# Column sums of a LayerNorm backward: from TensorE products per tile to running sums on GpSimd

## The chip, the cores and the metric

The kernel runs on one core of a Trainium2 chip. The metric is the device time of one execution in microseconds (us), here as the median of several runs. The engines are named as in the profile: PE is TensorE (PEld its weight loads), DVE is VectorE, ACT is ScalarE, POOL is GpSimd, SP is SyncE, which here only issues DMAs.

## The reference

One transformer-like block and its whole backward pass: a recurrent-memory attention (64 segments of 32 rows with 8 memory rows, 32 heads of 128) and a gated feed-forward part, each behind a LayerNorm whose shift, scale and gate come from a conditioning vector `c`.

```
mod = (silu(c) @ w_mod).reshape(c.shape[0], 6, 1, -1)
sa, ca, ga, sb, cb, gb = mod[:, 0], mod[:, 1], ...
h = layernorm(x) * (1 + ca) + sa
x = x + ga * A_ref(h, A_mem0, A_Wq, A_Wk, A_Wv, A_Wo)
h = layernorm(x) * (1 + cb) + sb
x = x + gb * B_ref(h, B_w_gate, B_w_up, B_w_down)
# outputs: x, and the gradients of all differentiable inputs
```

The part that matters here is the gradient of `sa` and `ca`. With `dh` the gradient of the first `h` (2048 rows of 512), they are sums over all rows: `dsa = sum(dh)` and `dca = sum(dh * xhat)`, where `xhat` is the normalised `x`. With the other four they make the six rows of `dmod`, from which the gradients of `w_mod` (output 11) and `c` (output 10) follow.

## The kernel before, in words

The kernel has phases 0 to 5. Phases 0 to 4 do the forward pass and the backward pass through the two parts. Phase 5 is the last stage: `phase5`, from about 2425 us to the end. It does two things side by side.

The first is the weight gradients of the attention. The list `todo` holds 36 chunks: 9 each for Wo, Wq, Wk and Wv, and each chunk covers `ng` = 4, 3, 4, 4, 3, 4, 4, ... heads (per group of 11, 11 and 10 heads: 4, 4 and 3, twice, then 4, 4 and 2). For Wo a chunk has one group of 20 products (128x128 by 128x512) for each head (L2195). For the other three a chunk has four groups of 20 products with `ng` x 128 columns (L2180). A group accumulates in one PSUM buffer out of six (`psG`, tag "p"), is evacuated by DVE and ACT in turn into one of three `ot` (or `ot5o`) buffers (L63 and L61 are the lines of the helper `evac`), and is stored by a DMA issued on POOL (L2184, L2200). The row tiles of a chunk, `rows5`, have three buffers; `load_rows(i + 2)` is issued in chunk `i`, on SP and ACT (L1984). Chunk 0's products were partly done at the end of phase 4 (L2002).

The second is the backward pass of the first LayerNorm in 16 tiles of 128 rows. `ln_load` loads `x0`, `dhb` and `dx1` on SP (two buffers each). `ln_tile(j)` computes the statistics on DVE, `rstd` on POOL (L2069), `xh` on DVE (L2071), the product `pr` = `dhb` * `xh` on POOL (L2074), the row gradient on DVE and ACT in `ln_bwd_rows` (L2219 to L2235), and its cast and store on POOL (L2078, L2079). `ln_step` calls it ahead of chunks 6 to 29, about two tiles for three chunks. The two column sums are made on PE: L2072 multiplies the whole `dhb` tile by `sel[:, 0, :]`, a 128x128 matrix whose column 0 is ones and whose other columns are zero, and L2075 does the same for `pr` with column 1. All 32 products accumulate in one PSUM tile, `acc_ps`, whose rows 0 and 1 then hold the sums.

From chunk 30 on `mod_grads` finishes: step 0 copies the two rows (`accs`, L2088), writes them to the DRAM tensor `DMOD` (L2089) and loads all of `DMOD` back, broadcast to 128 partitions (`dmod_bc`, L2091); steps 1 to 4 make `w_mod`'s gradient (L2098) and a dot product (L2101); step 5, ahead of chunk 35, makes `c`'s gradient (`dcb` L2111, a transpose on PE L2113).

The order on each engine is chosen when the kernel is built: the framework's scheduler goes by the order of the program, but may let an engine do a later instruction early if that one is ready in its model. So in the trace DVE and POOL work on a tile some tens of microseconds ahead of the chunk at which it stands in the program, while PE keeps the program's order. On SP the program's order is pinned up to chunk 5. Semaphore waits between engines, and those for the reuse of a buffer, are set by the framework. An engine works through its queue strictly in order, so an instruction that waits holds all behind it.

Of the kernel before, what the change touches and what calls it, by code (L numbers as in the profile page):

```python
# [7 lines left out]
BF16 = mybir.dt.bfloat16  # L8
F32 = mybir.dt.float32
AF = mybir.ActivationFunctionType  # L10
ALU = mybir.AluOpType
# [29 lines left out]
class K:  # L41
# [1971 lines left out]
    def phase5(self):  # L2013
        nc, tc, cfg, io = self.nc, self.tc, self.cfg, self.io
        D, DC, H, E, L, M, T, NS, NT, G = cfg.D, cfg.DC, cfg.H, cfg.E, cfg.L, cfg.M, cfg.T, cfg.NS, cfg.NT, cfg.G
# [6 lines left out]
        with ExitStack() as ctx:  # L2022
# [7 lines left out]
            wp = ctx.enter_context(tc.tile_pool(name="p5a_w", bufs=1, reuse_waits="tile"))  # L2030
# [1 line left out]
            sb2 = ctx.enter_context(tc.tile_pool(name="p5a_s2", bufs=2, reuse_waits="tile"))  # L2032
            psAcc = ctx.enter_context(tc.tile_pool(name="p5a_psAcc", bufs=1, space=PSUM, reuse_waits="tile"))
            ca1_bc = wp.tile([128, D], F32, name="ca1_bc")
            sel = wp.tile([128, 2, 128], BF16, name="sel5")
            nc.vector.memset(sel[:], 0.0)
            for i in range(2):
                nc.vector.memset(sel[:, i, i:i + 1], 1.0)
            mhalf = wp.tile([128, 1], F32, name="mhalf5")
            nc.gpsimd.memset(mhalf[:], -0.5)  # L2040
            acc_ps = psAcc.tile([128, D], F32, name="acc5_ps")

            ln_in = {}

            def ln_load(j):
                if j >= NT or j in ln_in:
                    return
                r0, r1 = j * 128, (j + 1) * 128
                x0 = sb2.tile([128, D], BF16, name="x0_5")
                nc.sync.dma_start(x0[:], x_rows[r0:r1, :])  # L2050
                dhb = sb2.tile([128, D], BF16, name="dhb5")
                self.load_x_rows(dhb, j, self.DHA, self.DHB)
                dx1 = sb2.tile([128, D], F32, name="dx1_5")
                nc.sync.dma_start(dx1[:], self.DX1ROWS[r0:r1, :])
                ln_in[j] = x0, dhb, dx1

            def ln_tile(j):
                r0, r1 = j * 128, (j + 1) * 128
                ln_load(j)
                ln_load(j + 1)  # L2060
                x0, dhb, dx1 = ln_in.pop(j)
                st = sb1.tile([128, 6], F32, name="st5")
                nc.vector.bn_stats(st[:], x0[:])
                mv = sb1.tile([128, 2], F32, name="mv5")
                nc.vector.bn_aggr(mv[:], st[:])
                ve = sb1.tile([128, 1], F32, name="ve5")
                nc.vector.tensor_scalar_add(ve[:], mv[:, 1:2], EPS)
                rstd = sb1.tile([128, 1], F32, name="rstd5")
                nc.gpsimd.tensor_tensor(rstd[:], ve[:], mhalf[:], op=ALU.pow)  # L2069
                xh = sb1.tile([128, D], F32, name="xh5")  # L2070
                nc.vector.tensor_scalar(xh[:], x0[:], mv[:, 0:1], rstd[:, 0:1], op0=ALU.subtract, op1=ALU.mult)  # L2071
                nc.tensor.matmul(acc_ps[:, :], lhsT=sel[:, 0, :], rhs=dhb[:], start=(j == 0), stop=False)  # L2072
                pr = sb2.tile([128, D], BF16, name="pr5")
                nc.gpsimd.tensor_tensor(pr[:], dhb[:], xh[:], op=ALU.mult)  # L2074
                nc.tensor.matmul(acc_ps[:, :], lhsT=sel[:, 1, :], rhs=pr[:], start=False, stop=(j == NT - 1))  # L2075
                dx0 = self.ln_bwd_rows(sb1, dhb, ca1_bc, xh, rstd, dx1, name="dx0")
                dx0b = sb2.tile([128, D], BF16, name="dx0b")
                nc.gpsimd.tensor_copy(dx0b[:], dx0[:])  # L2078
                nc.gpsimd.dma_start(dx0_rows[r0:r1, :], dx0b[:])  # L2079
# [4 lines left out]

            def mod_grads(step):
                if step == 0:
                    accs = sb1.tile([2, D], F32, name="accs5")
                    nc.vector.tensor_copy(accs[:], acc_ps[0:2, :])  # L2088
                    nc.sync.dma_start(self.DMOD[0:2, :], accs[:])  # L2089
                    mg["bc"] = sbm.tile([128, 6 * D], F32, name="dmod_bc")  # L2090
                    nc.sync.dma_start(mg["bc"][:], self.DMOD[:, :].rearrange("r d -> (r d)").partition_broadcast(128))  # L2091
                    mg["dscT"] = sbm.tile([128, DC], F32, name="dscT")
                elif step <= DC:
                    cc = step - 1
                    wm = sbm.tile([128, 6 * D], BF16, name="wmod5", bufs=2)
                    nc.sync.dma_start(wm[:], io["w_mod"][cc * 128:(cc + 1) * 128, :])
                    o = sbm.tile([128, 6 * D], BF16, name="dwm")
                    nc.scalar.activation(o[:], mg["bc"][:], AF.Copy, scale=self.scT[:, cc:cc + 1])  # L2098
                    nc.sync.dma_start(io["out_11"][cc * 128:(cc + 1) * 128, :], o[:])
                    junk = sbm.tile([128, 6 * D], BF16, name="junk5")  # L2100
                    nc.vector.scalar_tensor_tensor(out=junk[:], in0=wm[:], scalar=1.0, in1=mg["bc"][:], op0=ALU.mult,  # L2101
                                                   op1=ALU.mult, accum_out=mg["dscT"][:, cc:cc + 1])
                elif step == DC + 1:
                    t1 = sbm.tile([128, DC], F32, name="dc_t1")
                    nc.vector.tensor_scalar(t1[:], self.sigc[:], -1.0, 1.0, op0=ALU.mult, op1=ALU.add)
                    nc.vector.tensor_mul(t1[:], t1[:], self.cT[:])
                    nc.vector.tensor_scalar_add(t1[:], t1[:], 1.0)
                    nc.vector.tensor_mul(t1[:], t1[:], self.sigc[:])
                    nc.vector.tensor_mul(t1[:], t1[:], mg["dscT"][:])
                    dcb = sbm.tile([128, DC], BF16, name="dcb16")  # L2110
                    nc.vector.tensor_copy(dcb[:], t1[:])  # L2111
                    dc_ps = psT.tile([DC, 128], BF16, name="dc_ps")
                    nc.tensor.transpose(dc_ps[:, :], dcb[:, :], self.ident[:, :])  # L2113
                    dc_rows = sbm.tile([DC, 128], BF16, name="dc_rows")
                    nc.vector.tensor_copy(dc_rows[:], dc_ps[:])
                    nc.sync.dma_start(io["out_10"].rearrange("o (cc p) -> (o cc) p", p=128), dc_rows[:])
# [3 lines left out]
            def ln_step():  # L2120
                if ln_done[0] < NT:
                    ln_tile(ln_done[0])
                    ln_done[0] += 1

            if not getattr(cfg, "skip_wgrad", False):
# [35 lines left out]
                for i, (_, kind, outw, (hl, g0, ng)) in enumerate(todo):  # L2161
# [6 lines left out]
                    rows = loaded.pop(i)  # L2168
# [4 lines left out]
                    if i >= n_ln:  # L2173
                        mod_grads(i - n_ln)
                    h0 = 3 * g0 + hl
                    if kind == "qkv":
                        for c in range(DC):
                            ps = psG.tile([128, 4 * E], F32, name="gps5", tag="p")
                            for tp_ in range(NTP):
                                nc.tensor.matmul(ps[:, 0:ng * E], lhsT=hrows[:, tp_, c * 128:(c + 1) * 128],  # L2180
                                                 rhs=rows[:, tp_, 0:ng * E], start=(tp_ == 0), stop=(tp_ == NTP - 1))
# [4 lines left out]
                    else:  # L2186
# [4 lines left out]
                        else:  # L2191
                            pss = [psG.tile([128, D], F32, name="gps5o", tag="p") for _ in range(ng)]
                            for gg in range(ng):
                                for n, t in enumerate(self.p5_order):
                                    nc.tensor.matmul(pss[gg][:], lhsT=rows[:, t, gg * E:(gg + 1) * E], rhs=dyrows[:, t, :],  # L2195
                                                     start=(n == 0), stop=(n == NTP - 1))
# [202 lines left out]
```

## Time and profile before

| what | value |
|---|---|
| time, median of 3 runs | 3001.38 us (2998.03, 3001.38, 3002.9) |
| span of the profiled execution, first to last instruction | 2991.0 us |
| the median above that span | 10.4 us |
| mean granted clock of PE | 0.996 |
| PE busy, whole span | 2932.8 us (98%) |
| POOL busy, whole span | 1197.2 us (40%) |
| last stage, 2425 to 2991 us: PE, DVE, ACT, POOL busy | 558.37, 143.20, 63.26, 155.72 us |

No separate device time is given for the profiled execution; its span stands in for it, and the 10.4 us lie around it or between executions. In the rows of the profile "x" is a count, "128x512 bf16<-128x512 f32" the output and the input of an instruction, and what stands behind "<-" at the end of a row is what the engine had waited for. Names lack their buffer numbers, so `dhb5` stands as `dhb`, `ot5` as `ot`.

### The profile page before, as it was taken

The numbers are of one execution on the slowest core, as the hardware profiler recorded it, in microseconds if no ns is written. First come the engines' busy times: TensorE is split into PE (matmuls) and PEld (weight loads), VectorE is DVE, ScalarE is ACT, GpSimd is POOL, SyncE is SP. The second block draws the span as 40 slices with busy tenths as digits, with TensorE's granted clock in tenths as the row PEclk, the third lists the DMA queues.
The fourth block names the chain that finished last, engine by engine and source line by source line (L and its number), as shares of the span: only waits on it lengthen the run. The fifth ranks groups of instructions, "written<-read, shape, count | busy, mean of one in ns | idle before, by whom it ended". The sixth has DMA issues, their size and how long they took to land.

```text
span 2991.0 us, 105890 instructions
## 1 busy us (share of the span) xinstructions
PE 2932.8 (98%) x43975; PEld 1839.9 (62%) x44049; DVE 1612.4 (54%) x3679; ACT 1271.8 (43%) x3057; POOL 1197.2 (40%) x2456
## 2 busy tenths in 40 slices
PE   6999999999999999999999999999999999999999
PEld 3666666666665544445677777777777754445454
DVE  5566656666655788833456665566566532222230
ACT  2555555555555533312355555555555520011111
POOL 2454555555545222221344444444444422333321
PEclk8999999999999999999999999999999999999999
DMA  9898888889889899998699999999999997766574
GB/s 310 222 223 211 214 217 217 213 214 215 217 218 277 211 230 226 229 290 278 200 251 251 251 253 243 250 250 250 255 255 250 254 281 245 242 207 214 178 245 144
DMA packets 836438, 703.05 MB, mean 235 GB/s; under 512 B 536643, under 2 KB 708851, under 8 KB 835061
## 3 DMA queue, kind: packets, MB, share of 16 engines
q1 hardware_dynamic: 710756, 486.09, 65.5%
q0 software_dynamic: 54640, 148.90, 15.7%
q10 hardware_dynamic: 70560, 61.28, 6.5%
q8 instruction: 347, 5.69, 0.8%
q14 instruction: 135, 1.10, 0.1%
HBM read 294.99 MB, written 276.35 MB: 191 GB/s over the span
## 4 chain that ended last, share of the span: by engine, by line
PE 87%; issue 5%; DMA 3%; DVE 2%; POOL 1%; ACT 1%; SPq 1%; DVEq 0%; POOLq 0%; ACTq 0%
PE pass_ps L257 14%; PE gps L2180 9%; PE dh_ps L215 8%; PE pass_ps L659 5%; PE g_ps L1810 5%; PE gps5o L2195 4%; PE dhq_ps L223 4%; PE at_ps L223 4%; PE mm L1291 3%; PE dh_tps L215 3%; PE gps L1470 3%; PE turn_ps L829 2%; PE mm L1266 2%; PE mm L1251 1%; PE tps L1727 1%
## 5 line engine op out<-in xcount | busy, mean ns | idle before, releaser
L2180 PE MATMUL gps<-rows,hrows 128*128 128x512 bf16 (+2 forms) x2125 | 415.6, 355 | 1.8
L2180 PEld LDWEIGHTS <-hrows 128*128 128x128 bf16 x2160 | 211.3, 98 | 204.5
L61 ACT ACTIVATE ot<-gps 128x512 bf16<-128x512 f32 (+3 forms) x75 | 41.3, 550 | 362.2 <-PE gps L2180 229.1
L1855 POOL COPY dOst<-RAd 96x512 bf16<-96x512 bf16 x128 | 75.3, 613 | 297.8 <-DVE RAd L63 297.8
L1038 POOL TENSOR_TENSOR Pst<-Pst,rden 120x1408 bf16<-120x1408 bf16 x63 | 159.9, 2538 | 77.8 <-issue 49.6
L659 PE MATMUL pass_ps<-Wv,hT 128*32 128x512 bf16 (+2 forms) x2304 | 187.2, 358 | 0.0
L63 DVE CAST ot<-gps 128x512 bf16<-128x512 f32 (+3 forms) x76 | 48.1, 633 | 247.0 <-PE gps L2180 169.9
L2184 POOL DMA_DIRECT2D out_dram<-ot x108 | 81.5, 755 | 249.1 <-DVE ot L63 141.9
L257 PEld LDWEIGHTS <-hT 128*32 128x32 bf16 x4096 | 114.8, 97 | 103.9 <-issue 5.7
L63 DVE CAST Vst<-pass_ps 96x512 bf16<-96x512 f32 x128 | 87.3, 682 | 107.0 <-ACT RBv L61 98.5
L215 PE MATMUL dh_ps<-WvT,dVT 128*32 128x512 bf16 x2048 | 133.3, 380 | 1.7
L659 PE MATMUL pass_ps<-Wv,hb 128*32 128x512 bf16 (+2 forms) x636 | 128.7, 353 | 0.0
L257 PE MATMUL pass_ps<-Wq,hT 128*32 128x512 bf16 x2048 | 123.9, 383 | 4.8 <-DMA Wq<-in_A_Wq_dram 4.8
L257 PE MATMUL pass_ps<-Wk,hT 128*32 128x512 bf16 x2048 | 123.2, 382 | 2.5 <-POOL hT L549 1.1
L223 PE MATMUL at_ps<-Wo,OT 128*32 128x256 bf16 x4096 | 123.9, 273 | 0.7 <-DMA Wo<-in_A_Wo_dram 0.6
L257 PE MATMUL pass_ps<-WoT,dyT 128*32 128x256 bf16 (+1 forms) x3072 | 122.5, 308 | 0.9 <-ACT dyT L1936 0.9
L223 PE MATMUL dhq_ps<-WqT,dQT 128*32 128x256 bf16 x4096 | 122.9, 273 | 0.0
L215 PE MATMUL dh_ps<-WkT,dKT 128*32 128x512 bf16 x2048 | 122.3, 380 | 0.0
L794 POOL DMA_DIRECT2D Vst<-RBv x192 | 99.9, 526 | 55.6 <-ACT ET L841 34.4
L2195 PE MATMUL gps5o<-WoT,rows 128*128 128x512 bf16 x548 | 120.6, 379 | 1.0 <-DMA rows<-OSR 0.4
L223 PEld LDWEIGHTS <-dQT 128*32 128x32 bf16 x4096 | 109.7, 97 | 15.8
L315 DVE TENSOR_TENSOR dST<-dh_ps,dST 128x512 bf16<-128x512 f32 x64 | 44.3, 692 | 129.9 <-ACT dST L314 129.9
(471 smaller groups left out, 6991.2 us busy)
## 6 DMA issues: line engine op xcount, KB each, us to landing
OSR<-Ost SPq DMA_DIRECT2D x64, 352.0 KB
OT<-OT SPq DMA_DIRECT2D x64, 352.0 KB
PS<-Pst SPq DMA_DIRECT2D x64, 352.0 KB
Pst_l<-PS SPq DMA_DIRECT2D x64, 352.0 KB
OT_l<-OT SPq DMA_DIRECT2D x64, 352.0 KB
DVR<-rows_x POOLq DMA_DIRECT2D x64, 352.0 KB, 6.3
DKR<-rows_x POOLq DMA_DIRECT2D x64, 352.0 KB, 5.7
DQR<-rows_x POOLq DMA_DIRECT2D x64, 352.0 KB, 3.4
```

Of the source, the lines that this page charges most:

```text
L63: return nc.vector.tensor_copy(out, in_)
L215: self.nc.tensor.matmul(ps[32 * j:32 * j + 32, :], lhsT=lhsT, rhs=w, start=(n < 4), stop=(n >= total - 4), tile_position=(0, 32 * j))
L223: nc.tensor.matmul(ps[32 * j:32 * j + 32, :], lhsT=x[k], rhs=w[k][:, 256 * d:256 * d + 256], start=(n == 0), stop=(n == total - 1), tile_p ...
L257: self.nc.tensor.matmul(ps[32 * j:32 * j + 32, :], lhsT=lhs(c), rhs=rhs, start=(c == 0), stop=(c == DC - 1), tile_position=(0, 32 * j))
L659: nc.tensor.matmul(ps[32 * j:32 * j + 32, o * E:(o + n) * E], lhsT=lhsT, rhs=wc[:, 3 * a + hl:3 * (a + n - 1) + hl + 1:3, :], start=(c == ...
L794: nc.gpsimd.dma_start(Vst[96 + 8 * j:104 + 8 * j, :], rb[32 * j + o:32 * j + o + 8, :])
L1038: nc.gpsimd.tensor_tensor(Pst[0:120, :, :], Pst[0:120, :, :], rden[:, :].unsqueeze(2).to_broadcast([120, G, 128]), op=ALU.mult)
L1291: nc.tensor.matmul(hp[:], lhsT=xT[:, fc, :], rhs=wT[:, fc, :], start=(n == 0), stop=(n == 2 * FC - 1))
L1470: nc.tensor.matmul(ps[:], lhsT=h2r[:, j, c * 128:(c + 1) * 128], rhs=xr[:, j, :], start=(j == 0), stop=(j == NT - 1))
L1810: nc.tensor.matmul(ps[:, j, 0:w], lhsT=lh[:, g * GW:(g + 1) * GW], rhs=rh[:, g * GW:g * GW + w], start=True, stop=True)
L2180: nc.tensor.matmul(ps[:, 0:ng * E], lhsT=hrows[:, tp_, c * 128:(c + 1) * 128], rhs=rows[:, tp_, 0:ng * E], start=(tp_ == 0), stop=(tp_ == ...
L2195: nc.tensor.matmul(pss[gg][:], lhsT=rows[:, t, gg * E:(gg + 1) * E], rhs=dyrows[:, t, :], start=(n == 0), stop=(n == NTP - 1))
```

## The change

The sums are kept by POOL in one fp32 tile, `sums5` (128 partitions x 2 x 512), which is cleared at the start of the stage. In each of the 16 LayerNorm tiles POOL adds `dhb` to the first half and `pr` to the second, elementwise, and the two products on PE are left out. When all tiles are done, step 0 of `mod_grads` makes two fp32 products, which sum the 128 partitions: `sel` is now 128x2x2 in fp32, and the output has two rows. Everything else is as before.

```diff
-            sel = wp.tile([128, 2, 128], BF16, name="sel5")
+            sel = wp.tile([128, 2, 2], F32, name="sel5")
             nc.vector.memset(sel[:], 0.0)
             for i in range(2):
                 nc.vector.memset(sel[:, i, i:i + 1], 1.0)
+            sums = wp.tile([128, 2, D], F32, name="sums5")
+            nc.gpsimd.memset(sums[:], 0.0)
...
+            def add_rows(i, rows):
+                nc.gpsimd.tensor_tensor(sums[:, i, :], sums[:, i, :], rows[:], op=ALU.add)
...
                 nc.vector.tensor_scalar(xh[:], x0[:], mv[:, 0:1], rstd[:, 0:1], op0=ALU.subtract, op1=ALU.mult)
-                nc.tensor.matmul(acc_ps[:, :], lhsT=sel[:, 0, :], rhs=dhb[:], start=(j == 0), stop=False)
+                add_rows(0, dhb)
                 pr = sb2.tile([128, D], BF16, name="pr5")
                 nc.gpsimd.tensor_tensor(pr[:], dhb[:], xh[:], op=ALU.mult)
-                nc.tensor.matmul(acc_ps[:, :], lhsT=sel[:, 1, :], rhs=pr[:], start=False, stop=(j == NT - 1))
+                add_rows(1, pr)
                 dx0 = self.ln_bwd_rows(sb1, dhb, ca1_bc, xh, rstd, dx1, name="dx0")
...
                 if step == 0:
+                    for i in range(2):
+                        nc.tensor.matmul(acc_ps[0:2, :], lhsT=sel[:, i, :], rhs=sums[:, i, :], start=(i == 0), stop=(i == 1))
                     accs = sb1.tile([2, D], F32, name="accs5")
                     nc.vector.tensor_copy(accs[:], acc_ps[0:2, :])
```

## The prediction

> **What bounds the kernel now.** I read the page's first lines, then the windows view over the last stage, the groups by line there, TensorE's (PE's) order of time, the waits, and last the stores and evacuations that could hold PE up.
>
> ```profile
> span 2991.0 us, 105890 instructions
> PE 2932.8 (98%) x43975; PEld 1839.9 (62%) x44049; DVE 1612.4 (54%) x3679; ACT 1271.8 (43%) x3057; POOL 1197.2 (40%) x2456
> 2443.20:2977.00 533.80, 531.33 (x2624) 261.26 (x2672) 139.19 (x270) 60.70 (x86) 149.02 (x197) 1.00 0.67 219
> PE gps5o L2195 <- DMA rows<-OSR: 0.4, 1, 0.4
> ```
>
> The third line is the windows row of the last stage from chunk 1 to chunk 34: length, then busy time of PE, PEld, DVE, ACT, POOL, the granted clock (1.00), DMA share and GB/s. PE is busy 531.33 of 533.80 us; POOL (GpSimd) 149.02, that is 28%. The last line is the only wait of PE that the waits view lists for the stage. So here a product less on PE is time less, as long as nothing else falls behind.
>
> ```profile
> 2443.20 77.86 PE L2195 MATMUL gps5o<-WoT,rows 128*128 128x512 bf16 x353 [0.43 <-DMA rows<-OSR]
> 2520.89 0.38 PE L2072 MATMUL acc_ps<-dhb,sel 128*128 128x512 bf16 x1
> 2521.11 0.38 PE L2075 MATMUL acc_ps<-pr,sel 128*128 128x512 bf16 x1
> 2521.32 17.43 PE L2195 MATMUL gps5o<-WoT,rows 128*128 128x512 bf16 x78
> 2583.05 30.43 PE L2180 MATMUL gps<-rows,hrows 128*128 128x512 bf16 x158
> 2613.75 17.43 PE L2180 MATMUL gps<-rows,hrows 128*128 128x512 bf16 x78
> 2881.73 0.38 PE L2072 MATMUL acc_ps<-dhb,sel 128*128 128x512 bf16 x1
> 2881.95 0.38 PE L2075 MATMUL acc_ps<-pr,sel 128*128 128x512 bf16 x1
> 2882.16 95.23 PE L2180 MATMUL gps<-rows,hrows 128*128 128x384 bf16 x472
> ```
>
> These are rows of PE's order of time: start, length, line, operation, how many. From 2443.20 to 2520.89 stand chunks 1 to 5, 18 heads of 20 products: 77.69 / 360 = 0.2158 us from one 512-column product to the next. The 0.38 of a single row is its passage through the pipeline; the two sums products start 0.22 apart and the next weight-gradient product 0.21 later. So each of them takes one full place, 0.2158 us, in a queue that has no holes.
>
> **What is removed.** 16 tiles of 2 products, 32 x 0.2158 = 6.91 us, all between 2520.89 and 2882.16. Their weight loads ran beside other products and bring nothing more. VectorE's fills of `sel` become smaller by tenths of a microsecond at the stage's start, off PE; I count nothing for them.
>
> **What PE gets back.** Two fp32 products of 512 columns ahead of chunk 30. No fp32 product stands in this trace. Bounds: as cheap as a bf16 product, 2 x 0.2158 = 0.43; or, since this kernel itself carries an fp32 value as a high and a low bf16 part (`sc_parts`), high and low of both operands, so four bf16 products in one: 8 x 0.2158 = 1.73, and if none of the eight hides its passage, 8 x 0.38 = 3.04. I take 1.73, by the kernel's own way of carrying fp32, and keep 0.43 to 3.04 for the range. The Trainium skill, page "FP8 and Floating Point Precision", section "TensorE Precision Notes", says that true FP32 takes four passes through the array; by it the sum would be the same 1.73, and no row here shows such a product.
>
> Net on PE: -6.91 + 1.73 = **-5.18 us** (from -6.48 to -3.87).
>
> **What GpSimd gets.** Two additions of 128x512 into an fp32 tile per tile of rows, 32 in all, and one clearing of 128x1024 fp32.
>
> ```profile
> L2074 POOL TENSOR_TENSOR pr<-dhb,xh x16: 1166/1608/1692, 2459.8 to 2857.4; 128x512 bf16<-128x512 bf16 x16
> L1038 POOL TENSOR_TENSOR Pst<-Pst,rden 120x1408 bf16<-120x1408 bf16 x63 | 159.9, 2538 | 77.8 <-issue 49.6 <-DMA Pst<-ET 20.6 <-POOL hT L549 6.2
> L1857 POOL MEMSET Kst<- 128x1408 bf16 x1 | 1.3, 1277 | 0.0
> 2441.20 0.54 POOL L2200 DMA_DIRECT2D out_dram<-ot5o  x1 [7.59 <-DVE ot5o L63]
> ```
>
> The first row gives min/median/max of the nearest operation: same engine and width, one bf16 and one fp32 input. The second, all bf16, gives 2538 / 1408 = 1.80 ns a column, 0.92 us at 512. I take the median of the first, 1.61 us (0.92 to 1.69): 32 x 1.61 = 51.5 us, so POOL goes to about 200 of 534 us (38%). The clearing costs 0.9 (by columns) to 1.9 us (by bytes), from the third row; POOL stands idle 7.59 us before its first store of the stage, which covers it. If that cover were gone, the first store would come under 2 us later.
>
> So POOL's sum is far from PE's; what counts is who waits behind the additions. POOL also issues every store of an `ot`/`ot5o` tile. There are three such buffers, so evacuation k waits until store k-3 has landed, and PE may not start group k+6 before evacuation k (six PSUM buffers). I worked out for all 140 groups how long an evacuation could still be late; the tightest is the first of chunk 11, `ng`=3, 384 columns:
>
> ```profile
> 2611.98 0.69 DVE L2063 BATCH_NORM_STATS2 st<-x 128x6 f32<-128x512 bf16 x1 [5.38 <-DMA x<-in_A_x_dram]
> 2612.59 0.54 DVE L63 CAST ot<-gps 128x384 bf16<-128x384 f32 x1
> 2617.45 0.49 ACT L61 ACTIVATE ot<-gps 128x384 bf16<-128x384 f32 x1 [9.89 <-DMA out_dram<-ot]
> out_dram<-ot POOLq DMA_DIRECT2D x72, 128.0 KB, 3.5
> ACT ot L61 <- DMA out_dram<-ot: 25.3, 4, 9.9
> DVE ot L63 <- DMA out_dram<-ot: 14.8, 5, 4.7
> ```
>
> Chunk 10 began at 2583.05 and takes 80 x 0.2158 = 17.26, so that group ended at 2600.31 + 20 x 0.1619 = 2603.5 (384 columns: 0.2158 x 0.75); it was evacuated by 2613.1. Its buffer is wanted again two 512-column groups after 2613.75, at 2622.4. So 9.2 us were to spare. Per tile the additions put 3.2 us ahead of the stores behind them, 3.4 at the longest. That fits, and from chunk 12 on the spare time I found is 11 us or more.
>
> **VectorE beside it.** Its work on the same tile can be held too:
>
> ```profile
> L2223 DVE SCALAR_TENSOR_TENSOR dx_junk<-dx_dxh,xh x16: 693/1524/1528, 2461.6 to 2858.1; 128x512 f32<-128x512 f32 x16
> 2583.14 1.60 POOL L2074 TENSOR_TENSOR pr<-dhb,xh 128x512 bf16<-128x512 bf16 x1 [2.92 <-PE acc_ps L2072]
> 2583.76 1.52 DVE L2223 SCALAR_TENSOR_TENSOR dx_junk<-dx_dxh,xh 128x512 f32<-128x512 f32 x1
> ```
>
> The same instruction takes 0.69 us at best and 1.52 beside a POOL operation, ending just after it. Two more POOL operations can hold two more VectorE instructions by some 0.83 us each: 1.7 us. With the 3.4 an evacuation comes at most 5.1 us later, against 9.2 to spare. I price this at nothing on PE. The Trainium skill speaks against the change here: "SBUF — State Buffer", "SBUF: two separate sides", says that VectorE operations with two SBUF inputs and GpSimd share a port pair as an exclusive lock, held for the whole instruction. By it every such pair excludes each other, and the trace agrees (1.52 against 0.69); the sum stays as it is while 5.1 is below 9.2.
>
> **Waits that go.** The wait in the second row above (POOL on an old PE product of two tiles before, 2.92 us, and one of 2.5) goes, as `pr` and `dhb` are now read on POOL alone. That gives POOL 5 us back, not PE. The loads of `dhb` on SP's queue may start earlier, never later than POOL's own reading.
>
> **The end of the sums.**
>
> ```profile
> 2857.41 1.63 POOL L2074 TENSOR_TENSOR pr<-dhb,xh 128x512 bf16<-128x512 bf16 x1 [3.89 <-DMA dhb<-DHB]
> 2882.37 0.68 DVE L2088 COPY accs<-acc_ps 2x512 f32<-2x512 f32 x1 [4.00 <-PE acc_ps L2075]
> 2883.26 0.46 SPq L2089 DMA_DIRECT2D DMOD<-accs  x1
> 2890.59 0.35 SPq L2091 DMA_DIRECT2D dmod_bc<-DMOD  x1
> 2915.87 0.17 DVE L2111 CAST dcb<-dc_t 128x4 bf16<-128x4 f32 x1
> 2977.32 0.22 PE L2113 MATMUL dc_ps<-ident,dcb 128*4 128x128 bf16 x1
> 2987.09 0.72 POOL L2184 DMA_DIRECT2D out_dram<-ot  x1 [1.37 <-ACT ot L61]
> ```
>
> The last `pr` ends at 2859.0; with two additions and a store the sums are complete by about 2864. PE reaches chunk 30 at 2882.16 + 80 x 0.1619 = 2895.1, less 6.9: 2888.2. So PE doesn't wait for GpSimd (24 us to spare). The copy `accs` now follows at about 2890, 8 us later than now. Behind it on VectorE stand evacuations: an idle VectorE up to 2890 may hold one or two groups of 384 columns for up to 8 us, of 16 (five groups of 3.24) that PE may lead. On SP's queue the round trip through `DMOD` (7.3 us from 2883.26 to 2890.59) also moves 8 us back; behind it stand the row loads of chunks 33 to 35, the first wanted at 2942 (chunks 30 and 31, 17.3 us each, and 32, 12.95, after 2895.1). The four `w_mod` steps follow, and `dcb` would be ready at about 2924, against PE's use at 2977.3 - 5.2 = 2972. Nothing of it reaches the end: after PE's last group come one evacuation and one store, as now.
>
> So the span goes from 2991.0 to 2985.8. The shown runs have a median 10.4 us above the span of the profiled execution, which I leave as it is: 3001.38 - 5.18 = **2996.2 us**.
>
> **Rivals.**
> *A, stores fall behind (slower).* With three `ot` buffers the loop evacuation, store issue, landing must turn in three groups, 3 x 4.316 = 12.95 us. At the longest wait of 9.9 with 0.69 + 0.54 + 3.2 it takes 14.3: 1.4 us too long each time. If landings were that slow at all 16 tiles, 22 us would gather, 9.2 are absorbed: +13, less 5.2: about 3009; with VectorE held as well (1.7 a tile) 16 x 3.1 - 9.2 - 5.2 = +35: 3036. It decides from about 0.9 us a tile without recovery. For it: nine waits on stores are there today (25.3 + 14.8 us). Against: the median landing is 3.5 us, at which the loop takes 7.9, and lateness falls back. Chance 0.13, mostly near the lower price.
> *B, the changed queues cost PE directly (slower).* The larger tile moves all later tiles of the stage, and queues are filled anew; PE could find one `rows` load or evacuation late per few chunks. Price: a miss as large as A's spare, 9.2, once or twice: +4 to +13, 3005 to 3015. Nothing shown speaks for it. Chance 0.07.
> *C, the saving isn't kept (same).* PE is ahead by 6.9 us and then waits as long for a `rows` load, as it did once for 0.43 us. 3001.4. Against: one such wait in 36 chunks. Chance 0.07.
>
> **How the numbers follow.** The forecast has 0.73. About 0.2% (6.0 us, to 2995.4) is what a measurement of this kernel tells from no change; the forecast's -5.18 lies 0.8 us short of it, the fp32 price moves it by +-1.3, and the shown runs differ by 4.9 us (2998.03 to 3002.9). So it falls on both sides almost evenly: 0.36 faster, 0.37 same. C and the mild ends of A and B add 0.07 + 0.03 to same; the rest, 0.17, is slower. The forecast's own range is 2996.2 with -1.3/+1.3 for the price and 2.4 for the runs: 2992.5 to 2999.9. To hold 8 in 10 it takes in C and A's beginning: 2992 to 3005.
>
> **What would show it.** PE without L2072 and L2075 and with a short fp32 group of about 1.7 us ahead of chunk 30; chunks 6 to 29 back to back; POOL's additions near 1.6 us; a busy POOL near 200 us in the stage; `accs` near 2890. It is wrong if PE's waits list an evacuation (DVE or ACT `ot`) or if the fp32 group is above 3 us.

## The result, and the profile after

The changed kernel took 2994.05 us (median of 22 runs, 2986.64 to 3005.37), the kernel before beside it 2998.19 us (22 runs, 2993.78 to 3009.0). The ratio is 0.9985 with a 95% interval of 0.9978 to 0.9992: 4.5 us faster (2.4 to 6.6), where 5.18 were forecast.

One profile alone would have misled. The profiled execution with the change has a span of 2993.6 us, 2.6 us *longer* than the 2991.0 of before. PE's order of time shows where. First before, its last group; then the last stage with the change (start, length, line, operation, count):

```profile
2977.47 8.91 PE L2180 MATMUL gps<-rows,hrows 128*128 128x256 bf16 x80
```

```profile
2450.66 121.03 PE L2202 MATMUL gps5o<-WoT,rows 128*128 128x512 bf16 x549 [1.09 <-DMA rows<-OSR]
2571.52 324.36 PE L2187 MATMUL gps<-rows,hrows 128*128 128x512 bf16 x1652
2895.82 1.88 PE L2093 MATMUL acc_ps<-sums,sel 128*2 128x512 f32 x4
2897.63 82.24 PE L2187 MATMUL gps<-rows,hrows 128*128 128x512 bf16 x392
2979.80 0.22 PE L2120 MATMUL dc_ps<-ident,dcb 128*4 128x128 bf16 x1
2979.95 8.91 PE L2187 MATMUL gps<-rows,hrows 128*128 128x256 bf16 x80
```

Chunk 1 started 7.46 us later in this execution (2450.66 against 2443.20). From there to PE's last product, called the *stretch* below, it is 2443.20 to 2986.38 = 543.18 us before and 2450.66 to 2988.86 = 538.20 with the change: 4.98 less. The two sums products between the chunks are gone, chunks 6 to 29 stand back to back, and the fp32 pair takes 1.81 us of PE (2895.82 to 2897.63). The only wait of PE that the waits view lists for the stage is the 1.09 just ahead of the stretch.

GpSimd's new work and the tile's other operations, minimum/median/maximum in ns:

```profile
L2046 POOL TENSOR_TENSOR sums<-sums,dhb x16: 1149/1167/1725, 2467.1 to 2672.0; 128x512 f32<-128x512 f32 x16
L2046 POOL TENSOR_TENSOR sums<-sums,pr x16: 1482/1490/1499, 2470.9 to 2674.4; 128x512 f32<-128x512 f32 x16
L2079 POOL TENSOR_TENSOR pr<-dhb,xh x16: 1160/1289/1617, 2469.6 to 2673.1; 128x512 bf16<-128x512 bf16 x16
L2040 POOL MEMSET sums<- x1: 951/951/951, 2442.6 to 2442.6; 128x1024 f32 x1
L2237 DVE SCALAR_TENSOR_TENSOR dx_ta<-dx_dxh,rstd,dx x16: 741/1387/3140, 2469.5 to 2675.0; 128x512 f32<-128x512 f32 x16
```

The additions cost about what was forecast. But the last `pr` starts at 2673.1, where before it was 2857.4: the 16 tiles now bunch up in the first half of the stage. The waits for their loads, before and after, say the same:

```profile
DVE dx_dxh L2219 <- DMA dhb<-DHB: 65.3, 13, 9.7
```

```profile
DVE dx_dxh L2226 <- DMA dhb<-DHB: 10.7, 2, 7.5
```

So one tile's work follows the other's closely. The tightest evacuation shows what this does:

```profile
2652.95 3.07 DVE L2230 SCALAR_TENSOR_TENSOR dx_junk<-dx_dxh,xh 128x512 f32<-128x512 f32 x1
2653.19 1.16 POOL L2046 TENSOR_TENSOR sums<-sums,dhb 128x512 f32<-128x512 f32 x1
2654.30 1.16 POOL L2079 TENSOR_TENSOR pr<-dhb,xh 128x512 bf16<-128x512 bf16 x1
2655.54 1.50 POOL L2046 TENSOR_TENSOR sums<-sums,pr 128x512 f32<-128x512 f32 x1
2656.20 0.68 DVE L63 CAST ot<-gps 128x512 bf16<-128x512 f32 x1
```

This evacuation is that of the first group of chunk 13. That group ended at 2450.66 + 880 x 0.2158 = 2640.6 (860 places of chunks 1 to 12, then 20; from chunk 0 on, `ng` is 4, 4, 3, 4, 4, 3, 4, 4, 2). It was evacuated by 2656.9, and PE wanted the buffer at 2660.0, after three groups of 512 and two of 384 columns. Spare time: 3.1 us, against 9.2 for the tightest before. VectorE's `dx_junk`, 0.69 us when alone, was held for 3.07 us: it let two GpSimd operations pass and ended 0.48 us into the third.

### The profile page after: what moved, and what is told of

Its sections match the earlier page's. It is cut to its first block, busy times and chain, and to the rows that moved or that the text cites. A ratio compares the mean times of both kernels' runs of the same rounds, so it can differ in the third digit from the quotient of the medians.

```text
span 2993.6 us, 105831 instructions
## 1 busy us (share of the span) xinstructions
PE 2930.3 (98%) x43947; PEld 1838.7 (61%) x44021; DVE 1631.3 (54%) x3679; ACT 1271.0 (42%) x3057; POOL 1233.4 (41%) x2489
## 5 line engine op out<-in xcount | busy, mean ns | idle before, releaser
L2187 PE MATMUL gps<-rows,hrows 128*128 128x512 bf16 (+2 forms) x2124 | 413.6, 355 | 1.9
L2187 PEld LDWEIGHTS <-hrows 128*128 128x128 bf16 x2160 | 211.2, 98 | 204.4 <-issue 0.9
```

## The experiments

The theory: PE's places alone set the time (32 bf16 places out, one fp32 pair in), and the additions cost PE nothing as long as evacuations stay within their spare time. The rivals: the additions cost something through late stores and evacuations; the saving comes from elsewhere; the pair's price isn't fp32. A table of all runs, from the same views:

| kernel | stretch, us | tightest spare, us | last `pr` starts at | ratio to before (95%) |
|---|---|---|---|---|
| before | 543.18 | 9.2 | 2857 | 1 |
| the change | 538.20 | 3.1 | 2673 | 0.9985 (0.9978 to 0.9992) |
| ctrl_before | 543.19 | 9.2 | 2871 | one run |
| adds_only | 543.19 | 5.8 | 2866 | 1.000 (0.9991 to 1.0009) |
| no_adds | 536.28 | 10.3 | 2664 | 0.9983 (0.9972 to 0.9993) |
| bf16_final | 536.92 | 3.6 | 2666 | 0.9969 (0.9958 to 0.9981) |
| bf16_final_2 | 536.92 | 4.4 | 2666 | 0.9983 (0.9973 to 0.9992) |
| adds_x3 | 588.55 | none | 2723 | 1.016 (1.0145 to 1.0175) |
| adds_x3_braked | 554.97 | none | 2879 | 1.0045 (1.0027 to 1.0063) |
| braked | 541.82 | 6.0 | 2861 | 0.9995 (0.9986 to 1.0005) |
| adds_x3_dve | 538.20 | 7.1 | 2673 | 0.9983 (0.9974 to 0.9992) |
| bf16_final_dve | 536.91 | 10.4 | 2663 | 0.999 (0.9979 to 1.0002) |

**ctrl_before: the kernel before, once more.**

> The kernel before, profiled once more, to see what one profile is worth. Theory: the stretch from the start of chunk 1 to PE's last product is a count of places and repeats to 0.5 us (543.2 us); the time of day at which chunk 1 starts (2443.2 before, 2450.7 with the change) varies from run to run by several us, since it holds the start of the execution and earlier DMA waits. Rival: the start of chunk 1 repeats within 1 us, so the change itself moved it by 7.5 us.

```profile
2457.21 77.86 PE L2195 MATMUL gps5o<-WoT,rows 128*128 128x512 bf16 x360 [0.63 <-DMA rows<-OSR]
2991.49 8.91 PE L2180 MATMUL gps<-rows,hrows 128*128 128x256 bf16 x80
```

2457.21 to 3000.40: 543.19 us, the same to 0.01. Chunk 1 started 14 us later than in the first profile of the same program. The rival falls: two executions of one program differ by more than the 7.46 us ahead of the stage, and the stretch is the exact measure.

**adds_only: the additions beside the old products.**

```diff
+            sums = wp.tile([128, 2, D], F32, name="sums5")   # cleared, as in the change
                 nc.tensor.matmul(acc_ps[:, :], lhsT=sel[:, 0, :], rhs=dhb[:], ...)
+                add_rows(0, dhb)
                 nc.tensor.matmul(acc_ps[:, :], lhsT=sel[:, 1, :], rhs=pr[:], ...)
+                add_rows(1, pr)
```

> The additions and the clearing on GpSimd are there, the 32 products on PE stay, and the sums that GpSimd makes are not used. Theory (PE's places alone decide): stretch from chunk 1 to the last product 543.2 +-0.5 us, ratio to before 1.000 (+-0.001); tiles still spread out to about 2857 us, since PE's products still hold the buffers. Rival (the additions cost PE something through late stores): the stretch is longer by more than 1 us, up to 10.

```profile
2449.66 77.86 PE L2202 MATMUL gps5o<-WoT,rows 128*128 128x512 bf16 x360 [0.33 <-DMA rows<-OSR]
L2080 POOL TENSOR_TENSOR pr<-dhb,xh x16: 1171/1602/1612, 2468.6 to 2865.5; 128x512 bf16<-128x512 bf16 x16
```

Its last product ends at 2992.85, the stretch is 543.19: 32 additions cost PE nothing. The tiles stay spread out, so it isn't the additions that bunch them. The tightest evacuation is the one that the prediction looked at, the first of chunk 11, and it comes 3.4 us later than before (5.8 us to spare instead of 9.2).

**no_adds: the change without its additions.**

```diff
-                add_rows(0, dhb)
-                add_rows(1, pr)
```

> The change without its 32 additions (the two column sums are left out and come out as zero; the clearing and the two fp32 products stay). Theory: stretch 538.2 us as with the change, ratio 0.998 to 0.999; the LayerNorm tiles still bunch up early, before 2680 us, because what held them back were PE's products. Rival (the additions cost about 1 us on PE): stretch 537 or less. If the tiles spread out again, the bunching comes from the additions and not from the missing products.

```profile
2443.53 1.88 PE L2091 MATMUL acc_ps<-sums,sel 128*2 128x512 f32 x4
2452.26 121.03 PE L2200 MATMUL gps5o<-WoT,rows 128*128 128x512 bf16 x560
L2078 POOL TENSOR_TENSOR pr<-dhb,xh x16: 1157/1232/1685, 2468.9 to 2664.0; 128x512 bf16<-128x512 bf16 x16
```

With nothing to wait for, the scheduler put the pair ahead of chunk 1 (first row), so the stretch of 536.28 us lacks it. I had not foreseen that, and by the bare number the rival (537 or less) would hold; with the pair's 1.81 us the stretch is 538.1, as the theory has it. And 543.18 - 536.28 = 6.90 us is the price of the 32 products by themselves. The tiles bunch up without any addition: it is PE's missing products that let them. They read `dhb` and `pr`, so by the program a buffer came free, and SP's queue could go on to the next tile, only when PE reached that place. Without them the scheduler may also choose another order when the kernel is built; no run separates the wait from that choice.

**bf16_final, run twice: a bf16 pair at the end.**

```diff
+                    sumb = sb1.tile([128, 2, D], BF16, name="sumb5")
+                    nc.gpsimd.tensor_copy(sumb[:], sums[:])
-                        nc.tensor.matmul(acc_ps[0:2, :], lhsT=sel[:, i, :], rhs=sums[:, i, :], ...)
+                        nc.tensor.matmul(acc_ps[0:2, :], lhsT=sel[:, i, :], rhs=sumb[:, i, :], ...)   # sel in bf16
```

> As the change, but the sums are cast once to bf16 on GpSimd and the two products are bf16. Theory: the fp32 pair takes 1.81 us of PE, the bf16 pair 0.43 plus at most 0.3 of passage, so the stretch is 536.8 us (538.2 - 1.4), ratio 0.9975 to 0.9985. Rival (the pair's price is mostly switching between stages, not fp32): stretch 537.8 to 538.2.

> The bf16 pair once more, to tell its ratio (0.9969, 0.9958 to 0.9981 the first time) from what PE's places give. Theory: 536.9 us for the stretch again, 6.3 less than before, that is a ratio of 0.9979, within the interval; what was below it was scatter ahead of the stage. Rival (it gains more than PE's places): ratio at or below 0.997 again.

Here the pair of the change (its weight loads stand 0.43 us apart, two for each product), and that of this kernel:

```profile
2895.82 0.09 PEld L2093 LDWEIGHTS acc_ps<-sums,sel 128*2 128x2 f32 x2 [0.32 <-issue]
2896.25 0.08 PEld L2093 LDWEIGHTS acc_ps<-sums,sel 128*2 128x2 f32 x1 [0.34 <-issue]
2896.68 0.09 PEld L2093 LDWEIGHTS acc_ps<-sums,sel 128*2 128x2 f32 x1 [0.34 <-issue]
```

```profile
L2095 PE MATMUL acc_ps<-sumb,sel x2: 377/377/377, 2891.3 to 2891.5; 128*2 128x512 bf16 x2
2891.82 82.24 PE L2189 MATMUL gps<-rows,hrows 128*128 128x512 bf16 x400
```

The bf16 pair takes 0.53 us (2891.29 to 2891.82) instead of 1.81, and the stretch is 536.92 both times, 1.28 less than with the change: fp32 itself is the price. The ratio of 0.9969 was scatter for the most part; the second gave 0.9983, and PE's places give 1 - 6.26 / 2998 = 0.9979, inside both intervals. This is the best version I ran, ahead of the change by 1.3 us of PE's time, which the ratios can't separate.

**adds_x3: every addition three times.**

```diff
+                for _ in range(3):
+                    nc.gpsimd.tensor_tensor(sums[:, i, :], sums[:, i, :], rows[:], op=ALU.add)   # sel holds 1/3
```

> The change with each addition made three times (sel holds 1/3), so 64 more additions of 1.2 to 1.5 us on GpSimd, 5.3 us more for each of the 16 LayerNorm tiles. Theory (the late-stores rival is real but lies beyond the change): the tiles still bunch up, the tightest evacuation of the change had 3.1 us to spare, so PE now waits for evacuations around chunks 9 to 16; stretch from chunk 1 to the last product 540 to 552 us instead of 538.2. Rival (GpSimd is free enough whatever is put on it, 200 of 534 us): stretch 538.2, no wait of PE.

```profile
PE gps L2188 <- DVE ot L63: 17.6, 7, 3.9
PE gps L2188 <- DMA rows<-DQR: 9.1, 1, 9.1
PE gps L2188 <- ACT ot L61: 8.8, 1, 8.8
L2188 PE MATMUL gps<-rows,hrows 128*128 128x512 bf16 (+2 forms) x2124 | 427.5, 362 | 38.2 <-DVE ot L63 17.6 <-DMA rows<-DQR 9.1 <-ACT ot L61 8.8
2620.00:2680.00 60.00, 50.88 (x221) 23.31 (x223) 39.57 (x56) 5.32 (x8) 54.13 (x58) 0.89 0.58 174
2594.85:2600.34 5.49, 5.49 (x13) 1.93 (x13) 3.60 (x6) 0.00 (x0) 4.94 (x8) 0.50 0.94 308
```

The stretch is 588.55 us, 50.35 more than with the change and far above the 540 to 552 expected. 36.3 of it is idle time ahead of L2187/L2188 (38.2 against 1.9), and 13.9 is that PE was busy longer (427.5 against 413.6): in the three windows of 60 us with the waits the granted clock is 0.89 to 0.91, and in the 5.49 us behind the longest wait it is 0.50 (last row), with 13 products at 0.42 us each instead of 0.2158. So PE pays for a wait of several microseconds twice. Together 50.2. The additions make things late in two ways. The first, in VectorE's and GpSimd's order of time:

```profile
2599.10 7.37 DVE L2231 SCALAR_TENSOR_TENSOR dx_junk<-dx_dxh,xh 128x512 f32<-128x512 f32 x1
2599.21 1.16 POOL L2047 TENSOR_TENSOR sums<-sums,dhb 128x512 f32<-128x512 f32 x1
2600.32 1.16 POOL L2080 TENSOR_TENSOR pr<-dhb,xh 128x512 bf16<-128x512 bf16 x1
2601.44 1.15 POOL L2047 TENSOR_TENSOR sums<-sums,dhb 128x512 f32<-128x512 f32 x1
2602.55 1.14 POOL L2047 TENSOR_TENSOR sums<-sums,pr 128x512 f32<-128x512 f32 x1
2603.66 1.14 POOL L2047 TENSOR_TENSOR sums<-sums,dhb 128x512 f32<-128x512 f32 x1
2604.77 2.71 POOL L2047 TENSOR_TENSOR sums<-sums,pr 128x512 f32<-128x512 f32 x2
2608.55 0.67 DVE L63 CAST ot<-gps 128x512 bf16<-128x512 f32 x1
```

One VectorE instruction took 7.37 us while six GpSimd operations passed back to back (the last POOL row holds the sixth and the seventh), and the evacuation behind it in VectorE's queue waited. For that evacuation PE didn't have to wait; for these it did:

```profile
2591.93 0.81 ACT L2241 ACTIVATE dx_tb<-xh,dx_b,dx_c 128x512 f32<-128x512 f32 x1 [17.94 <-DVE dx_c L2236]
2664.91 0.55 DVE L2077 TENSOR_SCALAR xh<-x,mv,rstd 128x512 f32<-128x512 bf16 x1 [10.80 <-POOL rstd L2075]
2665.37 0.69 DVE L63 CAST ot<-gps 128x512 bf16<-128x512 f32 x1
2666.11 14.95 PE L2188 MATMUL gps<-rows,hrows 128*128 128x512 bf16 x59 [3.90 <-DVE ot L63]
DVE xh L2077 <- POOL rstd L2075: 50.8, 14, 10.8
```

In the first row ScalarE's `dx_tb` had waited 17.94 us for a result of VectorE, where two instructions were held in that time, for 7.80 and 7.28 us. Directly behind it ScalarE issued the `rows` load that PE waited 9.14 us for; the evacuation behind PE's wait of 8.8 us stood behind such a `dx_tb` too. The second way is in the other rows: VectorE's `xh` needs `rstd` from GpSimd, where it stood behind six additions. VectorE sat idle for 10.80 us, the evacuation came next in its queue, and PE waited 3.90. Four of PE's waits are of this kind, 14.8 us of the 36.3.

**braked and adds_x3_braked: the old hold on the buffers put back.** Both have, where the old products stood, two products of 2 columns that read `dhb` and `pr`; their result is overwritten. The second has the tripled additions too.

```diff
                 add_rows(0, dhb)
+                nc.tensor.matmul(acc_ps[0:2, 0:2], lhsT=one2[:], rhs=dhb[:, 0:2], start=True, stop=True)
...
                 add_rows(1, pr)
+                nc.tensor.matmul(acc_ps[0:2, 0:2], lhsT=one2[:], rhs=pr[:, 0:2], start=True, stop=True)
```

> The change with the same two 2-column products for each tile, additions as in the change. Theory: tiles spread to about 2857 us, the tightest evacuation has about 6 to 9 us to spare instead of 3.1, and the stretch is 539 to 541.5 us, so it gains nothing in time over the change (ratio 0.9985 to 0.9995). Rival: bunched as in the change.

> The same tripled additions, and for each tile two products of 2 columns on PE that read dhb and pr (their result is overwritten and not used), where the old sums products stood: they cost PE next to nothing but hold the two buffers until PE comes by, as the old products did. Theory (the missing products let the tiles bunch up): tiles spread out again to beyond 2820 us, no wait of PE, stretch 538.2 + 32 x 0.03 to 0.1 = 539 to 541.5 us. Rival (the scheduler's choice or the additions bunch them): the tiles end before 2750 us and PE waits as without the small products.

```profile
2446.62 77.86 PE L2206 MATMUL gps5o<-WoT,rows 128*128 128x512 bf16 x353 [0.42 <-DMA rows<-OSR]
2524.53 17.44 PE L2206 MATMUL gps5o<-WoT,rows 128*128 128x512 bf16 x78
L2082 POOL TENSOR_TENSOR pr<-dhb,xh x16: 1158/1608/1618, 2465.6 to 2860.9; 128x512 bf16<-128x512 bf16 x16
PE gps L2192 <- DVE ot L63: 9.1, 3, 5.7
```

The first three rows are of braked, the last of adds_x3_braked. The tiles spread out again in both, so PE's reading of the two tiles is what had spaced them. But a pair of tiny products costs 0.22 us (360 places end at 2446.62 + 77.69 = 2524.31), hence the stretch of 541.82, just above what I expected, and the spare time rose from 3.1 to 6.0 us, the low end of the 6 to 9 expected. Spacing took most of the loss away (588.55 to 554.97, of which 3.6 are the tiny products), but not all: PE still waited, against the theory. With tripled additions even a spaced tile makes evacuations late.

**adds_x3_dve: the tripled additions on VectorE.** The one edit to adds_x3:

```diff
-                    nc.gpsimd.tensor_tensor(sums[:, i, :], sums[:, i, :], rows[:], op=ALU.add)
+                    nc.vector.tensor_tensor(sums[:, i, :], sums[:, i, :], rows[:], op=ALU.add)
```

> The tripled additions, but on VectorE (0.7 us each by its other 512-column operations with two inputs) instead of GpSimd; nothing else differs from the tripled additions that cost 50 us. Theory (PE ran dry because VectorE's two-input instructions were held while GpSimd's additions stood back to back, 7.8 us for one of 0.74 us, and evacuations stand behind them): no wait of PE above 1 us, stretch from chunk 1 to the last product 538.2 to 539, one dx_ta below 2.5 us. Rival (96 more operations in the tiles' chain make evacuations late on whatever engine): waits of PE again, stretch above 545.

```profile
2442.22 121.03 PE L2203 MATMUL gps5o<-WoT,rows 128*128 128x512 bf16 x560 [1.14 <-DMA rows<-OSR]
L2047 DVE TENSOR_TENSOR sums<-sums,pr x48: 675/679/693, 2460.8 to 2677.3; 128x512 f32<-128x512 f32 x48
L2238 DVE SCALAR_TENSOR_TENSOR dx_ta<-dx_dxh,rstd,dx x16: 731/742/2209, 2465.9 to 2677.9; 128x512 f32<-128x512 f32 x16
```

The last product ends at 2980.42: a stretch of 538.20, the change's own, with three times its additions. The 50 us of adds_x3 came from where the additions ran, not from their number. Both ways of being late go with them (`xh` now waits 8.9 us in all for `rstd`, not 50.8), so how much of the 50 us belongs to each is not shown by a run.

**bf16_final_dve: the bf16 pair and single additions on VectorE** (the same one-word edit to bf16_final).

> The bf16 pair at the end, and the 32 additions on VectorE instead of GpSimd. Theory: PE's places are the same, so the stretch is 536.9 us and the ratio to before 0.998 (0.9972 to 0.9988) as with the additions on GpSimd; only the spare time of the tightest evacuation grows, from 3.6 us to above 6. Rival: VectorE, which also evacuates, becomes late: less than 3 us to spare, or a wait of PE.

The stretch is 536.91 and the tightest spare time 10.4 us, as the theory has it. The ratio, 0.999 (0.9979 to 1.0002), holds the expected 0.998 but doesn't by itself show a gain.

## Why the prediction was right

*PE's places.* 6.91 us were forecast for the 32 products; no_adds gives 6.90. The queue without holes was the right picture.

*The fp32 pair.* 1.73 forecast, 1.81 measured: 0.43 us for each of four records, and less than 0.1 for the end. An fp32 product takes the time of four bf16 places, as forecast; the trace shows it as two records of two places each, so that it is made of four partial products is inferred from the time alone.

*The sum.* -5.18 forecast, -4.98 in the stretch, -4.5 (-6.6 to -2.4) in the ratio. The absolute time, 2994.05 against 2996.2, is lower because the kernel before was too: 2998.19 over 22 runs instead of 3001.38 over three. The 10.4 us that I laid around the span were scatter: the profiled execution of the changed kernel took 2995.39 us at a span of 2993.6, so only 1.8 lie around it. That the absolute forecast came within 2.2 us is therefore partly luck; the difference is what the working gives. At 0.15% it lies short of the 0.2% that the prediction took as its mark for faster, and the interval of these 22 runs still excludes zero.

*GpSimd's additions.* 1.61 us each were forecast, 1.17 (`dhb`) and 1.49 (`pr`) measured, both within the bounds. POOL's busy time in the stage was to be near 200 us of 534; the windows row of the same stretch of time has 188.31, of which the additions are 44:

```profile
2443.20:2977.00 533.80, 530.29 (x2616) 260.04 (x2661) 160.75 (x272) 60.92 (x87) 188.31 (x233) 1.00 0.70 223
```

The clearing (0.95 us) and the end of the sums were covered as said: 24 us were to lie between the last addition and PE's pair, and as the tiles ran ahead it was 220 us (2675.9 to 2895.8).

*The spare time: right in its verdict, wrong in its size.* The step said that an evacuation comes at most 5.1 us later with 9.2 to spare, at least 4.1 left; 3.1 were left. Three things failed in it. It took the tiles' places in time from the trace of before, and said of `dhb` only that loads "may start earlier"; in fact the removed products were what spaced the tiles out. Where they stayed, in adds_only, the evacuation came 3.4 us later, well inside the 5.1. It let a VectorE instruction be held by one GpSimd operation, 0.83 us; it can be held by all that stand back to back, 3.07 us here and 7.37 with tripled additions. And it left out `xh`, which waits on VectorE for `rstd` on GpSimd: 17.9 us in all with the change against 3.4 before, most of it from the bunching (15.8 in no_adds, without an addition).

*The rivals.* A (stores and evacuations fall behind) didn't happen, but it is no fancy: three times the additions bring it at 50 us. It came through VectorE's instructions, held or waiting for `rstd`, and through what ScalarE had behind them, and not in the way by which I had priced it, the loop of three `ot` buffers: none of the evacuations that PE waited for had itself waited for a store just before. B and C left no trace: one wait of PE, 1.09 us, ahead of chunk 1, where it was 0.43 and 0.63 us in the two profiles of before.

## What to carry to other kernels

Where one engine's queue has no holes, a removed instruction is worth its place in the queue (here 0.2158 us, not the 0.38 of its row), and that can be checked to hundredths of a microsecond between two marks in the trace, while whole executions of one kernel scatter by 15 us and more. Before moving reads from the bound engine elsewhere, ask what those reads held: a consumer that releases buffers late also paces the producers, and without it their work bunches up. Work given to GpSimd is cheap for the bound engine only up to the point where back-to-back operations hold VectorE's two-input instructions, or delay a small result that VectorE waits for, with the evacuations behind; the same additions on VectorE had no such point here.

## What the runs showed of the hardware

A VectorE instruction with two inputs in SBUF isn't only delayed by the GpSimd operation that runs when it starts: it waited through six in a row, 7.37 us instead of 0.69 (it ended at 2606.47, in the seventh). The Trainium skill ("SBUF — State Buffer", "SBUF: two separate sides") describes a lock that whoever starts first holds for its whole instruction; the trace goes beyond that, since `dx_junk`, by the stamps of the profile, started at 2599.10, ahead of the first of the six at 2599.21, and ended behind six of them.

What let it in was a pause. By the stamps each of the six starts 0.03 to 0.05 us before the one ahead has ended; the seventh, which reads what the sixth wrote, starts 0.08 us after it (2605.99 against 2605.91), and `dx_junk` ended 0.48 us later. In the change it is the same: 2655.54 against 2655.46, and an end at 2656.02. In adds_x3, 11 of VectorE's instructions on the tiles took over 2 us. All of them ended 0.55 to 0.56 us after the end of an addition, nine times with such a pause of 0.08 us behind it and twice with the issue of a store; in one of them an earlier store's issue had not let it in. The `sums<-sums,pr` behind a pause took 1.48 to 1.50 us where VectorE was waiting (11 times in adds_x3) and 1.15 where it was not (6 times); in the change VectorE was waiting at all 16, and they took 1.49. So the longest holds came from GpSimd operations that don't need the result of the one just ahead.

An fp32 product of 128x512 by a weight of two columns took 0.86 to 0.91 us of PE, in two records of 0.43, against 0.2158 for a bf16 one. And waits of 3 to 9 us of PE within the stage brought the granted clock down, to 0.50 in the 5.49 us behind the longest and to 0.89 over 60 us; PE was busy 13.9 us longer for it, beside the 36.3 us of waiting.
